# Finishing the results of a gated MLP by rows, and interleaving the first two units of each token block

## The chip, the cores and the metric

The kernel runs on one core of one Trainium2 chip. Its engines work side by side, each with its own queue: PE (TensorE) multiplies matrices into the accumulation memory (PSUM, eight banks), DVE (VectorE) and ACT (ScalarE) work element by element, POOL (GpSimd) and SP (SyncE) here only issue transfers between the chip's main memory and the on-chip memory. The metric is the time of one execution in device microseconds. Before the change it is 699.53 us, the median of three runs (698.68 to 700.48).

## The reference, cut to what matters

```python
x  = A_x                                   # 1 x 2048 x 512
xn = layernorm(x)
a, b = xn @ dft_hid_re.T, xn @ dft_hid_im.T
s  = dft_seq_re @ a - dft_seq_im @ b       # 2048 x 2048 matrices
h  = relu(xn @ w1 + b1) ** 2               # w1: 512 x 1792
g  = silu(h @ w2 + b2)                     # w2: 1792 x 512
return x + s * g
```

The change lies in the last two lines: `h @ w2`, the silu, the product with `s` and the sum with `x`.

## The kernel before, in words

Every matrix is float32. Each is split into a high and a low part (`split`, lines 68 to 76: ACT writes the high part, DVE the difference), and a product is three matmuls: high by high, high by low, low by high. On top of that the matrices are cut into two by two pieces and multiplied with seven products instead of eight (`PRODUCTS`, line 48). The four pieces of the result are put together from the seven products by `combine` (line 256): ACT copies product 1, then four DVE operations add and subtract the others, reading PSUM.

The stages are: layer norm and the sequence transform (up to about 408 us, with the hidden transform `stage2`, whose result `s` goes to main memory as `Y`), then MLP1 (`hidden`, 28 units, 420 to 549 us), which writes its squared results to main memory (`HD`), then MLP2 (the last loop, from line 815), in which the change lies.

MLP2 has 28 units. Unit n is token block c = n // 7 (512 tokens) and pair p = n % 7 (256 rows of w2). A unit does the seven products of its pair, 42 matmuls of 128 x 128 by 256 columns, through `add(k, p)` and `outer` (line 616), where k is the number of the product. All seven pairs of a block add up in the same seven accumulators, which take seven PSUM banks; so a new block can write a bank only when the last block's `combine` has read it. Products 2, 5 and 4 start from the bias, which ACT writes into the bank (`bias`, line 610). The order of products is `ORDER` (line 50), in the first unit of a block `FIRST`, and `FIRST_LAST` in the last block (lines 52, 53).

The left operand of unit n, `ready[c, p]`, lies in one of three places (`sixth(5 + n % 3, 2)`), so it can be made only when unit n - 3 no longer reads its own. It takes three steps (`operand`, line 589), which `go` calls by name: `h5` is the next step of unit 5's operand. They are a load from `HD` by SP, three DVE operations (`sums_a`, line 227), and the split into high and low. In unit n, behind its matmuls, `go` does the split of n + 2, the sums of n + 4 and the load of n + 6 (line 858). All engines work strictly in the order in which the program writes these calls (`manual_schedule`).

The right operands, the seven pairs of w2 in split form, lie in the places `W2_HOME` (line 511). Pairs 0, 1 and 6 are split in place; 2 to 5 are loaded in split form (`load_w2`, line 514, called as `l2` to `l5`). Pair `SHIFTED` is loaded in two pieces, and its seventh block (product 4's) lies `LINE` = 16 elements further on than it would otherwise.

After pair 6 of a block, `combine` writes the four result pieces to one buffer `e` (tag "e", one copy; the last block has its own, `g1a`). During the next block, `finish` (line 644) takes them one by one: silu on ACT (line 654), the product with `s` on DVE (line 658, `times`, with tiles loaded by `load_fin`), and a transfer on POOL (line 649) which adds the piece to the output. The output has held `x` since much earlier. A piece is one quarter of the block, 256 rows by 256 columns. The next `combine` may write `e` only when all four transfers have landed. The last block doesn't use `finish`: its matmuls of pairs 4 to 6 run product by product (`rest`, line 873), each piece is finished as soon as its products are done, and SP stores it.

Of the kernel before, what the change touches and what calls it, by code (L numbers as in the profile page):

```python
# [10 lines left out]
ALU = mybir.AluOpType  # L11

P = 128
S, D, F = 2048, 512, 1792
NS, ND, NF = S // P, D // P, F // P
NJ, NP = NS // 2, NF // 2
CW = 256
NC = S // CW
TC = 512
NTC = S // TC  # L20
# [4 lines left out]
REST = NP - 3  # L25
# [23 lines left out]

ORDER = (1, 2, 6, 7, 5, 3, 4)  # L50

FIRST = (1, 2, 6, 4, 7, 5, 3)
FIRST_LAST = (1, 2, 5, 4, 6, 7, 3)

B_SLOT = {B11: 0, B22: 1, B21: 2, T1: 3, T3: 4, T2: 5, T4: 6}
W1_SLOT = {A11: 0, A12: 1, A22: 2, S3: 3, S1: 4, S2: 5, S4: 6}
# [6 lines left out]
def fnet_gated_kernel(ctx, tc, x, xt, ct, wd, w1, w2, b1, b2, out):  # L63
    nc = tc.nc
# [22 lines left out]
    def bank(tag, name):  # L87

        n = {"b3": 3, "b2": 2}.get(tag, 1)
        return acc.tile([P, n, 512], F32, tag=tag, name=name)  # L90

    def buf(tag, shape, name, dtype=F32, bufs=1):
        return pool.tile(shape, dtype, tag=tag, bufs=bufs, name=name)
# [414 lines left out]
            nc.sync.dma_start(b.bitcast(F32), W1D[p][:, :, 3:7])  # L508
            W1[p] = [a[:, :, n] for n in range(3)] + [b[:, :, n] for n in range(4)]

    W2_HOME = "xc0", "xc1", 2, 3, 4, "wd0", "wd1"
    SHIFTED = 5

    def load_w2(p):
        to = W2_HOME[p]
# [94 lines left out]
    def bias(m, n, cols=slice(0, 2)):  # L610

        m = m.rearrange("p (k e) -> p k e", k=2)[:, cols]
        b = BIASED[n] * 256
        nc.scalar.activation(m, b2s[:, None, b:b + 256].to_broadcast([P, cols.stop - cols.start, 256]), AF.Copy)  # L614
# [13 lines left out]
    def at(src, k):  # L628

        h, b = WHERE[k]  # L630
        return src.rearrange("(h k p) (b e) -> h b p k e", h=2, k=2, b=2)[h, b]
# [9 lines left out]
                    nc.sync.dma_start(t[:, i].rearrange("p (k e) -> p k e", k=2), at(src, 2 * m + i))  # L641
                fin[c].append(t)

    def finish(c, e, k):

        silu(e, k)
        times(c, e, k)
        z = e[:, k].rearrange("p (k e) -> p k e", e=256)
        nc.gpsimd.dma_start(at(out[c * TC:(c + 1) * TC], k), z, accum_op=ALU.add)

    def silu(e, k, cols=slice(0, 2)):

        z = e[:, k, cols.start * 256:cols.stop * 256]
        nc.scalar.activation(z, z, AF.Silu)

    def times(c, e, k, cols=slice(0, 2)):
        w = slice(cols.start * 256, cols.stop * 256)
        nc.vector.tensor_tensor(e[:, k, w], e[:, k, w], fin[c][k // 2][:, k % 2, w], op=ALU.mult)
# [22 lines left out]
    for c, j in steps:  # L681
# [19 lines left out]
        if j == NJ - 1:  # L701
            e = buf("e", [P, 4, 512], f"c{c}")
# [4 lines left out]
        if c == NC - 1:  # L707

            if j == 2:
                e = buf("e", [P, 8, 256], "rows0")  # L710
# [24 lines left out]
    def go(*names):  # L735


        for v in names:
            k, n = v[0], int(v[1:])
            if k == "m":  # L740
                load_rows(n, buf("g1a" if n == 1 else "pq00", [P, 4, 256], f"rows{n}"))
            elif k == "l":
                load_w2(n)
            elif k != "h" or n < len(units):
                if v not in making:
                    making[v] = {"h": lambda: operand(n, *units[n]), "x": lambda: tokens(n // 2, n % 2),
                                 "w": lambda: late_w2(n)}[k]()
                next(making[v])
# [4 lines left out]
    def plan(c, p, ahead=(), behind=()):  # L753
        for n, names in enumerate((ahead, behind)):
            beside.setdefault((c, p), ([], []))[n].extend(names)
# [20 lines left out]
    plan(2, 6, ["h3"], ["h2"])  # L776
    plan(3, 0, [], ["w0"])
    plan(3, 1, ["w1", "l2"], ["h3"])
    plan(3, 2, ["l3"], ["w1"])
    plan(3, 3, [], ["w1"])  # L780
    plan(3, 4, ["l4", "w6"], ["h0"])
    plan(3, 5, ["h4"], ["h1"])
    plan(3, 6, ["h5"])

    with ordered:
        before = None
        for n, (c, p) in enumerate(units):
            ahead, behind = beside.get((c, p), ((), ()))
            go(*ahead)
            unit = hidden(n, c, p)  # L790
            next(unit)
            if n == 0:
                go("m1", "x2", "x3")
                for v in range(4, NP):
                    load_w1(v)
            if n == len(units) - 1:

                m26, m4 = bank("b2", "m_b2_o0"), bank("ba", "m_ba_o0")
                bias(m26[:, 0], 2)
                bias(m4[:, 0], 4)  # L800
            if before:
                next(before)
            next(unit)
            go(*behind)
            before = unit
            if n == 0:
                go(*["x2", "x3"] * 2)
                stage2(NC - 1, 0)
                stage2(NC - 1, 1, "ba")
                go("x2", "x3")  # L810
        m753, m1 = bank("b3", "m_b3_o0"), bank("bb", "m_bb_o0")
        bias(m753[:, 1], 5)
        next(before)

        for n, (c, p) in enumerate(units):
            last = c == NTC - 1
            if n == 0:
                ms = m26, m753, m4[:, 0], m1[:, 0]
                at_ = product
            elif not last and p == 0:  # L820

                m4, m26, m753, m1 = (bank(tag, f"m_{tag}_o{c}") for tag in (("bb", "ba")[c - 1], "b2", "b3", "bc"))
                ms = m26, m753, m4[:, 0], m1[:, 0]
                bias(ms[2], 4)
                bias(product(ms, 2), 2)
                bias(product(ms, 5), 5)
            elif p == 0:

                m5, m40 = (bank(tag, f"m_{tag}_last")[:, 0] for tag in ("bb", "bc"))
                m12, m67 = bank("b2", "m_12"), bank("b3", "m_67")  # L830
                m3 = bank("ba", "m_ba_last")[:, 0]
                m4 = m40, m67[:, 2]
                ms = {1: m12[:, 0], 2: m12[:, 1], 6: m67[:, 0], 7: m67[:, 1], 5: m5, 3: m3}
                at_ = dict.__getitem__
                bias(m5, 5)
                bias(m40, 4, slice(0, 1))
                bias(ms[2], 2)
                bias(m4[1], 4, slice(1, 2))

            def add(k, p):  # L840
                if last and k == 4:
                    for i in range(2):
                        outer(m4[i], k, ready[c, p], p, (i,))
                else:
                    outer(at_(ms, k), k, ready[c, p], p)

            go(*["l5"] * (n == 0))
            if not last or p < REST:
                for k in ORDER if p else FIRST_LAST if last else FIRST:
                    add(k, p)  # L850
            if n == 1:

                nc.scalar.activation(stats[:, 0, 0, 0:1], stats[:, 0, 0, 0:1], AF.Silu)
            if p == NP - 1 and not last:
                e = buf("e", [P, 4, 512], f"z{c}")
                combine(e, ms)
                done_next = c, e
            go(f"h{n + 2}", f"h{n + 4}", *["w6"] * (n in (0, 3)), f"h{n + 6}")
            if p == (3 if last else 5):
                load_fin(c)  # L860
            if p == NP - 1 and not last:
                done = done_next
            elif c:
                for k in ((2, 3), (0,), (1,), (), (), (), ())[p] if not last else ((), (0,), (1, 2), (3,), (), (), ())[p]:
                    finish(*done, k)


        e = buf("g1a", [P, 4, 512], f"z{c}")
        tail = NP - 1
        whole = slice(0, 512)  # L870
        w = [slice(i * 256, (i + 1) * 256) for i in range(2)]

        def rest(ks, ps=range(REST, NP)):
            for k in ks:
                for f in ps:
                    add(k, f)

        def step(to, a, b, op, w=whole):
            nc.vector.tensor_tensor(e[:, to, w], a[:, w], e[:, b, w], op=op)

        rest((1, 2, 6), range(REST, tail))
        rest((1, 2), (tail,))
        nc.scalar.activation(e[:, C21], ms[1], AF.Copy)
        step(C11, ms[2], C21, ALU.add)
        silu(e, C11)
        times(c, e, C11)
        plus(c, e, C11)
        rest((6,), (tail,))
        rest((7,))
        step(C22, ms[6], C21, ALU.add)  # L890
        step(C21, ms[7], C22, ALU.subtract)
        rest((5,))
        step(C12, m5, C22, ALU.subtract)
        step(C22, m5, C21, ALU.add)
        silu(e, C22)
        rest((3,))
        for f in range(REST, NP):
            outer(m4[0], 4, ready[c, f], f, (0,))
        times(c, e, C22)
        plus(c, e, C22)  # L900
        step(C12, m3, C12, ALU.add)
        silu(e, C12)
        step(C21, m4[0], C21, ALU.subtract, w[0])
        silu(e, C21, one)
        for f in range(REST, NP):
            outer(m4[1], 4, ready[c, f], f, (1,))
        times(c, e, C12)
        step(C21, m4[1], C21, ALU.subtract, w[1])
        silu(e, C21, two)
        times(c, e, C21, one)  # L910
        plus(c, e, C21, one)
        times(c, e, C21, two)
        plus(c, e, C21, two)
        plus(c, e, C12)
# [43 lines left out]
```

## Time and profile before

| | |
|---|---|
| median of three runs | 699.53 us (698.68 to 700.48) |
| the profiled execution | 698.08 us |
| its span, first to last instruction | 696.3 us |
| PE busy / DVE / ACT / POOL | 683.0 / 578.3 / 345.4 / 16.9 us |
| mean granted clock of TensorE | 0.997 |
| chain of waits, by engine | PE 89%, DVE 7%, issue 1%, DMA 1%, ACT 1% |
| MLP2, first matmul to last | 549.3 to 689.0 us |

The span is what lies between the first and the last instruction of one execution; the rest of the run's time lies outside. Engine times are busy times. In a row of a timeline come the start in us, the length in us, the engine, the line of the kernel, the operation, output <- input, the shape and how many instructions were merged into the row; in brackets how long the engine had been idle ahead of it, and what ended the wait. A row of transfers gives the count, the size of one, and the us from issue to landing.

### The profile page before, as it was taken

The numbers are of one execution on the slowest core, as the hardware profiler recorded it, in microseconds if no ns is written. First come the engines' busy times: TensorE is split into PE (matmuls) and PEld (weight loads), VectorE is DVE, ScalarE is ACT, GpSimd is POOL, SyncE is SP. The second block draws the span as 40 slices with busy tenths as digits, with TensorE's granted clock in tenths as the row PEclk, the third lists the DMA queues.
The fourth block names the chain that finished last, engine by engine and source line by source line (L and its number), as shares of the span: only waits on it lengthen the run. The fifth ranks groups of instructions, "written<-read, shape, count | busy, mean of one in ns | idle before, by whom it ended". The sixth has DMA issues, their size and how long they took to land.

```text
span 696.3 us, 12737 instructions
## 1 busy us (share of the span) xinstructions
PE 683.0 (98%) x5179; PEld 646.3 (93%) x5179; DVE 578.3 (83%) x866; ACT 345.4 (50%) x463; POOL 16.9 (2%) x20
## 2 busy tenths in 40 slices
PE   8999999999999999999999999999999999989995
PEld 5778889999999999999999989999999999989995
DVE  7998974579599598798797797989988699969885
ACT  3444634344353444444543326685867855344441
POOL 0000000000000000000000000000000100202011
PEclk9999999999999999999999999999999999999998
DMA  8622340734673763744835999374488954667674
GB/s 326 232 92 92 134 167 33 257 127 146 201 285 136 260 227 119 283 156 148 305 101 175 402 377 289 124 292 177 162 292 318 363 213 152 156 155 170 180 190 91
DMA packets 52250, 141.09 MB, mean 203 GB/s; under 512 B 4912, under 2 KB 18736, under 8 KB 50992
## 3 DMA queue, kind: packets, MB, share of 16 engines
q1 hardware_dynamic: 44896, 122.46, 50.5%
q10 hardware_dynamic: 3456, 12.58, 4.5%
q0 software_dynamic: 3840, 5.24, 4.3%
q8 instruction: 40, 0.66, 0.4%
q14 instruction: 18, 0.15, 0.1%
HBM read 97.00 MB, written 46.42 MB: 206 GB/s over the span
## 4 chain that ended last, share of the span: by engine, by line
PE 89%; DVE 7%; issue 1%; DMA 1%; ACT 1%; POOL 0%; DVEq 0%; ACTq 0%; POOLq 0%
PE m_b L322 23%; PE yps L309 13%; PE hps L573 10%; PE pq_b L375 7%; PE m_b_o L621 7%; PE hps_b L573 5%; PE m_bb L322 5%; PE m_ba L322 5%; PE m L621 3%; PE hps_ba L573 3%; PE pq_ba L375 2%; DVE block L72 1%; PE hps_bb L573 1%; PE pq_bb L375 1%; PE m_ba_o L621 1%
## 5 line engine op out<-in xcount | busy, mean ns | idle before, releaser
L322 PE MATMUL m_b<-g,block 128*128 128x256 f32 x1080 | 129.0, 276 | 0.0
L322 PEld LDWEIGHTS m_b<-g,block 128*128 128x128 f32 x1080 | 125.5, 188 | 0.1
L69 ACT ACTIVATE g<-raws 128x768 fp32r<-128x768 f32 (+2 forms) x65 | 57.4, 885 | 89.7 <-PE m_b L322 45.8
L72 DVE TENSOR_TENSOR g<-raws,g 128x768 fp32r<-128x768 f32 (+2 forms) x65 | 65.6, 1009 | 40.1 <-ACT g L69 40.0
L309 PE MATMUL yps<-wd,pq 128*128 128x512 f32 (+1 forms) x414 | 92.8, 374 | 0.0
L309 PEld LDWEIGHTS yps<-wd,pq 128*128 128x128 f32 x414 | 74.4, 188 | 13.7
L72 DVE TENSOR_TENSOR g<-sums,g 128x1024 fp32r<-128x1024 f32 x48 | 58.7, 1223 | 12.2 <-ACT g L69 12.2
L573 PE MATMUL hps<-xT,block 128*128 128x256 f32 x504 | 59.1, 276 | 0.0
L69 ACT ACTIVATE g<-sums 128x1024 fp32r<-128x1024 f32 x48 | 50.4, 1049 | 16.6 <-PE m_ba L322 7.8
L573 PEld LDWEIGHTS hps<-xT,block 128*128 128x128 f32 x504 | 58.0, 188 | 0.0
L375 PE MATMUL pq_b<-g,block 128*128 128x512 f32 x180 | 47.4, 395 | 0.5 <-DVE g L72 0.4
L621 PE MATMUL m_b_o<-w,block 128*128 128x256 f32 x360 | 43.9, 278 | 2.3 <-ACT m_b_o L614 2.3
L322 PE MATMUL m_b<-g,xc 128*128 128x256 f32 x360 | 45.0, 276 | 0.0
L621 PEld LDWEIGHTS m_b_o<-w,block 128*128 128x128 f32 x360 | 42.3, 188 | 2.8 <-ACT m_b_o L614 2.7
L322 PEld LDWEIGHTS m_b<-g,xc 128*128 128x128 f32 x360 | 42.8, 188 | 0.1
L375 PEld LDWEIGHTS pq_b<-g,block 128*128 128x128 f32 x180 | 33.3, 188 | 9.6 <-DVE block L72 2.1
L573 PE MATMUL hps_b<-xT,block 128*128 128x256 f32 x288 | 34.7, 276 | 0.0
L223 DVE TENSOR_TENSOR sums<-raws 128x512 f32<-128x512 f32 x49 | 33.7, 688 | 0.9 <-DMA raws<-in_ct 0.6
L69 ACT ACTIVATE block<-hr 128x1792 fp32r<-128x1792 f32 (+1 forms) x15 | 23.8, 1587 | 21.1 <-PE m_bb_o L621 6.5
L584 ACT ACTIVATE raws<-raws,b1s 128x512 f32<-128x512 f32 x42 | 28.1, 716 | 12.0 <-DVE raws L264 11.9
L573 PEld LDWEIGHTS hps_b<-xT,block 128*128 128x128 f32 x288 | 33.6, 188 | 0.0
L621 PE MATMUL m_b_o<-block 128*128 128x256 f32 x270 | 32.5, 278 | 0.0
(232 smaller groups left out, 1212.3 us busy)
## 6 DMA issues: line engine op xcount, KB each, us to landing
raws<-in_ct SPq DMA_DIRECT2D x63, 512.0 KB, 3.5
w1d<-w0g SPq DMA_DIRECT2D x21, 512.0 KB, 3.3
block<-w1d SPq DMA_DIRECT2D x6, 1792.0 KB, 9.1
hd<-raws ACTq DMA_DIRECT2D x18, 512.0 KB, 4.9
hr<-hd SPq DMA_DIRECT2D x15, 512.0 KB, 4.6
block<-w2d SPq DMA_DIRECT2D x3, 1792.0 KB, 15.5
y<-ysb SPq DMA_DIRECT2D x16, 256.0 KB, 3.2
fin<-y SPq DMA_DIRECT2D x16, 256.0 KB, 5.4
```

Source lines behind the costliest of these rows:

```text
L69: nc.scalar.activation(hi, src, AF.Copy)
L72: return nc.vector.tensor_tensor(lo, src, hi.bitcast(F32), op=ALU.subtract)
L223: nc.vector.tensor_tensor(t[:, 0:2], r[:, 0:1].to_broadcast([P, 2, 256]), r[:, 1:3], op=ALU.add)
L309: nc.tensor.matmul(ps[:, s], PQ[c, m, k // 2][:, a_, w:w + P], WD[m, k][:, b_, s], start=n == 0, stop=n > len(todo) - 3, skip_group_check= ...
L322: nc.tensor.matmul(ps[:, d * CW:(d + 1) * CW], w[:, a_, d * P:(d + 1) * P], mv(b_), start=first and d == 0 and (a_, b_) == (HI, HI), stop= ...
L375: nc.tensor.matmul(accs[c][k], w, g[:, b_, 2 * h:2 * h + 2], start=j == 0 and h == 0 and (a_, b_) == (HI, HI), stop=j == NJ - 1 and h == 1 ...
L573: nc.tensor.matmul(product(ms, k), W1[p][a][:, a_, q * P:(q + 1) * P], xT[c, q][:, b_, b], start=share not in first, stop=q == 1 and (a_, ...
L584: nc.scalar.activation(x_[:, s], x_[:, s], AF.Relu, bias=b1s[:, f:f + 1])
L621: nc.tensor.matmul(m[:, k * 256:(k + 1) * 256], g[:, a_, a, k * P:(k + 1) * P], W2[p][b][:, b_], start=p == 0 and k == 0 and (a_, b_) == ( ...
```

## The change

Three edits, all in MLP2.

*Order of products.* The first two units of a block are taken together, by `GROUPS`. A block's entry lists groups of products. In unit 0 only the first group is done, with pair 0; in unit 1 the first group with pair 1, and then each further group with pair 0 and with pair 1. Block 0 has the groups (1, 2, 6, 4), (7, 5, 3); blocks 1 and 2 have (1, 4), (2, 6), (7, 5, 3); block 3 has (5), (1, 2), (4, 6, 7, 3). At the end of a block the split of the operand after next (`h{n + 2}`) is called ahead of `combine`; for the last block the bank of product 5 gets its bias there too.

*Results by rows.* `finish` takes two pieces at a time, those of the same 256 rows, in units 1 and 2 of the next block. After their silus and products it issues two transfers, each of 128 whole rows (512 columns). So there still are four accumulating transfers of 256 KB for a block, on POOL. Before, pieces 2 and 3 were finished in unit 0, 0 in unit 1 and 1 in unit 2 (in the last block: 0 in unit 1, 1 and 2 in unit 2, 3 in unit 3).

*Shifted block.* The pair in two pieces with the shifted block is now pair 3, which takes the place `wd0`; pairs 4 and 5 move to the places 3 and 4. `wd0` becomes free only at the end of MLP1, so pair 3 is loaded at the start of MLP2 (`l3` where `l5` was), and pairs 4 and 5 during MLP1 where 3 and 4 were.

```diff
-FIRST = (1, 2, 6, 4, 7, 5, 3)
-FIRST_LAST = (1, 2, 5, 4, 6, 7, 3)
+GROUPS = ((1, 2, 6, 4), (7, 5, 3)), *[((1, 4), (2, 6), (7, 5, 3))] * 2, ((5,), (1, 2), (4, 6, 7, 3))
...
-    W2_HOME = "xc0", "xc1", 2, 3, 4, "wd0", "wd1"
-    SHIFTED = 5
+    W2_HOME = "xc0", "xc1", 2, "wd0", 3, 4, "wd1"
+    SHIFTED = 3
...
-    def finish(c, e, k):
-
-        silu(e, k)
-        times(c, e, k)
-        z = e[:, k].rearrange("p (k e) -> p k e", e=256)
-        nc.gpsimd.dma_start(at(out[c * TC:(c + 1) * TC], k), z, accum_op=ALU.add)
+    def finish(c, e, h):
+
+        for k in (2, 0) if h == 0 else (1, 3):
+            silu(e, k)
+            times(c, e, k)
+        for k in range(2):
+            n = c * TC + (1 - h) * 256 + k * P
+            nc.gpsimd.dma_start(out[n:n + P].rearrange("p (b e) -> p b e", b=2), e[:, h:4:2, k * 256:(k + 1) * 256],
+                                accum_op=ALU.add)
...
-    plan(3, 2, ["l3"], ["w1"])
+    plan(3, 2, ["l4"], ["w1"])
...
-    plan(3, 4, ["l4", "w6"], ["h0"])
+    plan(3, 4, ["l5", "w6"], ["h0"])
...
-                m5, m40 = (bank(tag, f"m_{tag}_last")[:, 0] for tag in ("bb", "bc"))
+                m40 = bank("bc", "m_bc_last")[:, 0]
...
-                bias(m5, 5)
...
-            go(*["l5"] * (n == 0))
-            if not last or p < REST:
-                for k in ORDER if p else FIRST_LAST if last else FIRST:
+            go(*["l3"] * (n == 0))
+            if p < 2:
+                groups = GROUPS[c]
+                for k in groups[0]:
+                    add(k, p)
+                for ks in groups[1:] if p else ():
+                    for f in (0, 1):
+                        for k in ks:
+                            add(k, f)
+            elif not last or p < REST:
+                for k in ORDER:
                     add(k, p)
...
             if p == NP - 1 and not last:
+                go(f"h{n + 2}")
+                if c == NTC - 2:
+                    m5 = bank("bb", "m_bb_last")[:, 0]
+                    bias(m5, 5)
                 e = buf("e", [P, 4, 512], f"z{c}")
                 combine(e, ms)
                 done_next = c, e
-            go(f"h{n + 2}", f"h{n + 4}", *["w6"] * (n in (0, 3)), f"h{n + 6}")
+            go(*[f"h{n + 2}"] * (p < NP - 1 or last), f"h{n + 4}", *["w6"] * (n in (0, 3)), f"h{n + 6}")
...
-                for k in ((2, 3), (0,), (1,), (), (), (), ())[p] if not last else ((), (0,), (1, 2), (3,), (), (), ())[p]:
-                    finish(*done, k)
+                if p in (1, 2):
+                    finish(*done, p - 1)
```

## The prediction

> **What bounds the kernel now.** I read the page first, then the chain of waits, then the timeline of each engine over MLP2 (549 us to the end), since every edit lies there.
>
> ```profile
> span 696.3 us, 12737 instructions
> ...
> 611.71 6.21 DMA out<-z
> 618.53 1.69 ACT block L69
> 621.28 1.64 PE m_b_o L621 x12
> ```
>
> In MLP2 the chain is mostly PE's matmuls, but at 611.71 it leaves PE for a result transfer of 6.21 us, and comes back only at 621.28. PE's timeline shows what that cost, and two more losses:
>
> ```profile
> 549.33 0.84 PE L621 MATMUL m_bb_o<-w,block 128*128 128x256 f32 x6
> ...
> 552.93 2.32 PE L621 MATMUL m_b_o<-w,block 128*128 128x256 f32 x18 [0.72 <-ACT m_b_o L614]
> ...
> 586.45 2.39 PE L621 MATMUL m_b_o<-w,block 128*128 128x256 f32 x18
> ...
> 599.27 3.70 PE L621 MATMUL m_b_o<-block 128*128 128x256 f32 x30
> ...
> 614.11 3.56 PE L621 MATMUL m_b_o<-w,block 128*128 128x256 f32 x30
> ...
> 618.68 0.97 PE L621 MATMUL m_bc_o<-w,block 128*128 128x256 f32 x6 [0.33 <-ACT z L261]
> 621.28 1.64 PE L621 MATMUL m_b_o<-w,block 128*128 128x256 f32 x12 [1.62 <-ACT m_b_o L614]
> ...
> 635.68 3.56 PE L621 MATMUL m_b_o<-block 128*128 128x256 f32 x30
> ...
> 656.62 2.03 PE L621 MATMUL m<-w,block 128*128 128x256 f32 x15
> ...
> 688.17 0.87 PE L621 MATMUL m<-w,block 128*128 128x256 f32 x6
> ```
>
> One matmul lasts 0.28 us and the next starts before its end, so 30 in 3.56 us are 29 steps of 0.1133; 30 in 3.70 are steps of 0.118. The slow step holds from 586.45 to about 614.1 and from 656.62 to the end, each time from a pause of under 0.3 us on; after the pauses at 552.93 and 621.28, over 0.6 us, the step is the quick one. In block 1 the slow step ends where the shifted weight block (pair 5, product 4) has been used. A unit of 42 matmuls is 4.76 us quick, 4.94 slow. PE ends at 688.17 + 0.87 = 689.04; 28 quick units without a pause from 549.33 would end at 682.6.
>
> Now the result transfers on POOL, with DVE's last products of the first pair ahead of them, the landing of the first, and two copies on the same queue (their line is 586):
>
> ```profile
> 540.24 0.71 POOL L586 DMA_DIRECT2D hd<-raws  x1 [539.79 <-ACT raws L585]
> 544.99 0.56 POOL L586 DMA_DIRECT2D hd<-raws  x1 [4.04 <-ACT raws L585]
> ...
> hd<-raws POOLq DMA_DIRECT2D x1, 512.0 KB, 9.1
> ...
> 593.32 1.29 DVE L658 TENSOR_TENSOR z<-z,fin 128x512 f32<-128x512 f32 x2
> ...
> 594.36 1.25 POOL L649 DMA_DIRECT2D out<-z  x1 [38.31 <-DVE z L658]
> 600.64 1.20 POOL L649 DMA_DIRECT2D out<-z  x1 [5.03 <-DVE block L72]
> ...
> out<-z POOLq DMA_DIRECT2D x1, 256.0 KB, 6.0
> ```
>
> Both products are done at 594.61, and yet the second transfer starts at 600.64, 0.28 us after the first has landed (594.36 + 6.0). The copies don't do this: the second is issued at 544.99, while the first lands at 549.3. I read it so that an accumulating transfer keeps POOL's queue until it has landed. Releasers given for these rows (a DVE split) are not it: what the transfer needs was there.
>
> ```profile
> 611.71 1.18 POOL L649 DMA_DIRECT2D out<-z  x1 [4.03 <-issue]
> 631.20 1.19 POOL L649 DMA_DIRECT2D out<-z  x1 [18.30 <-DVE z L658]
> ...
> 644.63 1.19 POOL L649 DMA_DIRECT2D out<-z  x1 [3.35 <-issue]
> 668.26 1.20 POOL L649 DMA_DIRECT2D out<-z  x1 [22.44 <-DVE z L658]
> ...
> 683.21 1.19 POOL L649 DMA_DIRECT2D out<-z  x1 [3.21 <-DVE z L658]
> ...
> out<-z POOLq DMA_DIRECT2D x1, 256.0 KB, 5.5
> ...
> out<-z POOLq DMA_DIRECT2D x1, 256.0 KB, 4.6
> ```
>
> A set of four so takes, first issue to last landing: 611.71 + 6.21 - 594.36 = **23.6** us; 644.63 + 5.5 - 631.20 = **18.9**; 683.21 + 4.6 - 668.26 = **19.6**. Mean 20.7. Until the set has landed its buffer z is taken, and the next block's combine cannot begin:
>
> ```profile
> 618.03 0.60 ACT L261 ACTIVATE z<-m_bc_o 128x512 f32<-128x512 f32 x1 [7.74 <-DMA out<-z]
> 650.25 0.60 ACT L261 ACTIVATE z<-m_bc_o 128x512 f32<-128x512 f32 x1 [3.89 <-PE m_bc_o L621]
> ...
> 618.66 1.23 DVE L262 TENSOR_TENSOR z<-m_b_o,z 128x1024 f32<-128x1024 f32 x1 [4.79 <-ACT z L261]
> ...
> 623.19 2.02 DVE L72 TENSOR_TENSOR block<-raws,block 128x1792 fp32r<-128x1792 f32 x1
> 625.12 0.69 DVE L229 TENSOR_TENSOR hr<-hr 128x512 f32<-128x512 f32 x1
> ...
> 626.64 2.02 DVE L72 TENSOR_TENSOR block<-sums,block 128x1792 fp32r<-128x1792 f32 x1
> ...
> 672.42 2.02 DVE L72 TENSOR_TENSOR block<-hr,block 128x1792 fp32r<-128x1792 f32 x1
> ```
>
> From these, start to start: copy to combine 0.63, combine 4.53, a split 1.93, the sums of one operand 1.52. Two result products take 1.2 by the row at 593.32. DVE works a whole unit's 3.45 us out of 4.76, and around a combine it is late.
>
> **The change part by part.** *Interleaving.* No matmul is added or taken away. In block 0 products 7, 5 and 3 come 24 matmuls later, so the pause of 0.72 goes: with its restart 1.0 us. Blocks 1 to 3 start with products whose banks are free first, and the short pauses at 586 and 656 go, and with them the slow step: 27.5 x 0.0047 / 0.118 = 1.1 us, and 32.4 us by the same share, 1.3 us. The 1.62 at 621.28 is covered by 12 more matmuls (1.36) ahead of it. With the 0.33 and the restarts, all that interleaving can give is 689.04 - 682.9 (28 units and the last matmul's length) = 6.1 us. It asks the second operand of a block earlier; moving that split ahead of the combine (on DVE 1.93, on ACT 1.7) supplies it, and makes the combine begin later.
>
> *Shifted block.* One pair 3 load now is due at unit 3 and not unit 5:
>
> ```profile
> 549.56 1.30 SPq L524 DMA_DIRECT2D w<-w2d  x2
> ...
> w<-w2d SPq DMA_DIRECT2D x1, 1536.0 KB, 10.6
> ```
>
> It lands at about 560.2; unit 3 starts at 549.33 + 3 x 4.76 = 563.6, so it is hidden by 3.4 us (the smaller second piece feeds only product 4, 4.1 us later). Without that cover it costs what it is late. The loads of pairs 4 and 5 start on SP's queue where those of 3 and 4 did, and are due later: nothing. Where a slow step does set in, it now ends two units sooner (0.4 us), and in block 3 at all.
>
> *Finishing by rows.* Activations, products and bytes stay. The first transfer of a set now waits for two products, in unit 1 of the block and not unit 0: that is later. The transfer's shape, 128 rows of two 1 KB pieces, has no row here; I bound it by 18.9 and 23.6 a set and take the mean, since number, bytes and queue are the same and I see no reason that the queue is released earlier. The Trainium skill speaks against that reading: "DMA: Bandwidth & Descriptors", section "Two DMAs through the same engine are not ordered", has descriptors of one queue start in order but pipelined. By that rule a second transfer would follow at once, and the sum would be that of the first rival; the two rows at 594.36 and 600.64 disagree.
>
> **The sum.** DVE before the first combine ends a sum at 580.6 (old combine 581.24 after 0.61 idle). Split 582.5, combine 587.1, then sum, split, sum, split, sum, two products: 3 x 1.52 + 2 x 1.93 + 1.2 = 9.6, so 596.7. Transfer 0.4 later: **597.1**, against 594.36. Set: 617.8. Copy 617.9, where it was 618.03. Combine 618.5 to 623.1; 9.6 and 0.4: second set from 633.1 (was 631.20) to **653.8**. Old: 650.1, and the copy at 650.25 waited for PE, not for the set; now it waits for the set. PE starts block 2 at 618.6 and without the 1.62 pause finishes at 651.9; product 5 of two units (12 matmuls) covers to 653.3, then it waits for the combine's first step, 653.9 + 0.63 + 1.23 = 655.8: 2.5 us. That is where the stall goes. Combine ends at 659.1. From there DVE has four sums, four splits and four products up to the operand of pair 5: 6.1 + 7.7 + 2.4 = 16.2, so 675.3 (old: 672.42 + 2.02 = 674.4). PE arrives after 8 of the last 126 matmuls, at about 674.4, and waits 0.9. Then 118 x 0.1133 + 0.28 = 13.7: **689.0**, as before. After PE nothing changes (its last products go through DVE in the same order). The profiled execution is 698.08, 1.45 under the median of 699.53; a change of 0.0 puts the median at **699.5**.
>
> What interleaving wins on PE is so held back by two sets of four transfers in a row. The end moves by the sum of both sets: 1 us a set is 2 us. So the landing time of a transfer decides, and with it what else is loading:
>
> ```profile
> 600.63 0.32 SPq L598 DMA_DIRECT2D raws<-hd  x1
> ...
> 644.92 0.32 SPq L598 DMA_DIRECT2D sums<-hd  x1
> ```
>
> Loads issued next to the transfers at 600.64 and 644.63, which both needed 5.5 us; the median of all is 4.7.
>
> **The rivals.** *1, the queue isn't held* (other pieces, or the hold was something else). Both sets land long before they matter, PE runs through: 682.9, gain 6.1, **693.4**. For it: the copies. Against: every transfer of the three sets starts as the one before lands. *2, quick sets.* With 18.9 both, 3.6 us come off: **696.0**. For: whole rows of 2 KB lie together; two of three sets are under 20. Against: the later start puts the third transfer of each set beside a load (splits end, and loads start, at 603.7 and 607.2 by my sum, the third transfer at about 607). *3, slower: each transfer of both sets meets loads*, as in the first set. With 23.6 both, 5.8 come on top: **705.3**. It decides from 21.7 a set (2.1 us in all). For: the fourth of each set falls beside the loads of the next results. Against: only one set of three was so long. The idle time at block 2 would be 5.4 us. The Trainium skill, "TensorE: Matmul & The Clock Gate", section "What's actually happening", halves the clock after an idle window of about 3.4 us; no pause in MLP2 here is so long, and it would add to this rival alone. *4, the slow step stays.* If the new order leaves short pauses, four units a block at 0.18 us more: up to 2.2 us, **701.7**, if they lie where PE is the bound.
>
> **How the numbers follow.** About 0.3% (2.1 us) is what a measurement of this kernel can tell from no change. Forecast 0.42; rival 1 0.13; 2 0.22; 3 0.18; 4 0.05. Faster: rivals 1 and 2, 0.35. Slower: 3 and half of 4, 0.21. The forecast's own range is 697.4 to 701.6; with rivals 1 and 2 whole and the milder part of 3, 693.0 to 704.0.
>
> **What will show it.** Rows of POOL: if two accumulating transfers of a set overlap, rival 1; the set's length from first issue to last landing, against 20.7, says 2 or 3. ACT's copy rows of blocks 1 and 2: both should end on the transfer, at 618 and 654. PE's row of block 3 should show a pause of 2 to 3 us after product 5, and one near 1 us at the operand of pair 5. Groups of 30 should read 3.56 throughout. A first transfer before 595, or a combine that doesn't wait, would make the prediction wrong.

## The result, and the profile after

The changed kernel takes **705.51 us** (median of six runs, 704.22 to 708.54); the kernel before, run beside it, 700.00 (six runs, 698.62 to 701.62). The ratio is 1.0085, with a 95% interval of 1.0062 to 1.0109: slower, by about 6 us. The forecast was 699.5 and no change; the result lies above its upper bound of 704.0 and at the number of rival 3 (705.3). In the profiled executions the time went from 698.08 to 705.54 us. In the changed kernel the product loop is line 620, the transfer line 650, ACT's copy line 260.

The page of the changed kernel, its span and its chain of waits:

```profile
span 703.8 us, 12738 instructions
...
PE 76%; DVE 14%; DMA 4%; issue 4%; ACT 2%; POOL 0%; DVEq 0%; ACTq 0%; POOLq 0%
```

PE had 89% of the chain before. Now DVE, transfers and "issue" have 22% together: the end is set in part by something else than matmuls. PE's timeline of MLP2 shows where:

```profile
549.73 0.84 PE L620 MATMUL m_bb_o<-w,block 128*128 128x256 f32 x6
...
585.81 6.96 PE L620 MATMUL m_b_o<-w,block 128*128 128x256 f32 x60
607.61 3.56 PE L620 MATMUL m_b_o<-block 128*128 128x256 f32 x30
620.64 1.58 PE L620 MATMUL m_bc_o<-w,block 128*128 128x256 f32 x6 [4.03 <-ACT z L260]
...
632.88 3.70 PE L620 MATMUL m_b_o<-block 128*128 128x256 f32 x30
...
662.23 4.34 PE L620 MATMUL m<-w,block 128*128 128x256 f32 x24 [4.33 <-ACT m L613]
...
696.01 0.52 PE L620 MATMUL m<-w,block 128*128 128x256 f32 x3
```

Blocks 0 and 1 run without a pause. The starts of blocks 2 and 3 wait for over 4 us each, and both rows behind a wait are far too long: six matmuls took 1.58 us where six otherwise take 0.84. The table by stretches gives the granted clock. A row has the stretch, its length, the busy time and count of PE, its weight loads, DVE, ACT and POOL, and then three numbers: granted clock, DMA share, GB/s.

```profile
620.60:624.20 3.60, 3.56 (x17) 3.56 (x18) 3.44 (x3) 1.09 (x2) 0.00 (x0) 0.53 0.00 0
624.20:632.00 7.80, 7.80 (x68) 7.80 (x68) 5.94 (x10) 4.04 (x4) 0.00 (x0) 1.00 0.25 68
...
662.20:664.90 2.70, 2.67 (x12) 2.67 (x13) 2.56 (x4) 0.68 (x2) 0.00 (x0) 0.50 0.00 0
```

After each pause the clock is at half (0.53, 0.50) for some 3 us, then full again. That is the rule which the prediction set beside rival 3 (the Trainium skill, "TensorE: Matmul & The Clock Gate", section "What's actually happening": half the clock after an idle window of about 3.4 us); the trace agrees, with waits of 4.03 and 4.33 us (rows above).

What the pauses wait for is in ACT's timeline, the copy at each block's start:

```profile
620.00 0.60 ACT L260 ACTIVATE z<-m_bc_o 128x512 f32<-128x512 f32 x1 [6.45 <-DMA out<-z]
...
659.69 0.60 ACT L260 ACTIVATE z<-m_bc_o 128x512 f32<-128x512 f32 x1 [5.74 <-DMA out<-z]
```

It is the last transfer of a set. POOL's timeline, then the us from issue to landing of the transfers at 607.02, 613.55 and 652.67, then SP's loads beside them:

```profile
597.73 1.14 POOL L650 DMA_DIRECT2D out<-z  x1 [41.27 <-DVE z L660]
602.37 1.09 POOL L650 DMA_DIRECT2D out<-z  x1 [3.50 <-issue]
607.02 1.09 POOL L650 DMA_DIRECT2D out<-z  x1 [3.56 <-issue]
613.55 1.07 POOL L650 DMA_DIRECT2D out<-z  x1 [5.44 <-issue]
637.09 1.09 POOL L650 DMA_DIRECT2D out<-z  x1 [22.47 <-DVE z L660]
...
652.67 1.08 POOL L650 DMA_DIRECT2D out<-z  x1 [5.26 <-issue]
```

```profile
out<-z POOLq DMA_DIRECT2D x1, 256.0 KB, 6.2
out<-z POOLq DMA_DIRECT2D x1, 256.0 KB, 6.3
...
out<-z POOLq DMA_DIRECT2D x1, 256.0 KB, 6.9
```

```profile
607.45 3.78 SPq L597 DMA_DIRECT2D hr<-hd  x2
611.28 2.64 SPq L640 DMA_DIRECT2D fin<-y  x4
...
651.16 1.97 SPq L640 DMA_DIRECT2D fin<-y  x4
```

The first two transfers of both sets needed 4.2 to 4.4 us. The first set lasts 613.55 + 6.3 - 597.73 = 22.1 us, the second 652.67 + 6.9 - 637.09 = **22.5** (forecast 20.7 each). The long ones stand beside loads: the fourth of each set starts within 2.3 us after four loads of `s` (`fin`, 1 MB), which `load_fin` issues in unit 5. The third of each (6.2 and 6.0 us) stands beside an operand's loads (`hr`).

**Where PE's time went.** From the start of each matmul to the next, all that lies above the quick step of 0.1133 us, summed over MLP2 and sorted by the length of the step; an experiment's row is explained below:

| kernel | last matmul starts | pauses (over 0.25 us) | steps of 0.19 to 0.25 us: half clock, and one restart behind each pause | slow steps (0.118) |
|---|---|---|---|---|
| before | 688.8 | 3.3 us | 0.6 us | 2.4 us |
| changed | 696.2 | 9.2 | 2.8 | 1.3 |
| rows alone | 698.6 | 9.7 | 4.1 | 2.2 |
| changed, loads of `s` later | 688.2 | 4.6 | 0.3 | 0.2 |
| order alone | 683.2 | 0 | 0 | 0.2 |
| changed, eight half transfers | 682.7 | 0 | 0.1 | 0.2 |

Changed against before: 0.4 later start + 5.8 of pauses + 2.2 in the half clock's column - 1.0 of slow steps = 7.4 us, which is the difference of the first column. The columns are not independent causes: time that PE loses in block 2 can shorten the wait at block 3.

### The profile page after: what moved, and what is told of

Read it like the earlier page. It is cut to its first block, busy times and chain, and to the rows that moved or that the text cites. A ratio compares the mean times of both kernels' runs of the same rounds, so it can differ in the third digit from the quotient of the medians.

```text
span 703.8 us, 12738 instructions
## 1 busy us (share of the span) xinstructions
PE 684.7 (97%) x5179; PEld 648.1 (92%) x5179; DVE 578.7 (82%) x866; ACT 346.1 (49%) x463; POOL 15.6 (2%) x20
## 4 chain that ended last, share of the span: by engine, by line
PE 76%; DVE 14%; DMA 4%; issue 4%; ACT 2%; POOL 0%; DVEq 0%; ACTq 0%; POOLq 0%
PE m_b L321 21%; PE yps L308 12%; PE hps L572 9%; PE pq_b L374 7%; PE hps_b L572 5%; PE m_bb L321 4%; PE m_ba L321 4%; DVE block L71 4%; PE m L620 3%; PE hps_ba L572 3%; DMA out<-z 2%; PE pq_ba L374 2%; DMA raws<-in_xt 1%; PE pq_bb L374 1%; PE hps_bb L572 1%
```

## The experiments

Beside these runs the kernel before took 698.1, 698.7 and 697.2 us on the three occasions (13, 27 and 24 runs); ratios are to it. **Theory A**: the four accumulating transfers follow one another, late and beside loads, and their length sets the end. **Rivals**: the new order, the shifted block, or the slow matmuls have a cause of their own.

### One part at a time

*Order and shift, finishing as before* (`finish` itself as it was, too).

```diff
-                if p in (1, 2):
-                    finish(*done, p - 1)
+                for k in ((2, 3), (0,), (1,), (), (), (), ())[p] if not last else ((), (0,), (1, 2), (3,), (), (), ())[p]:
+                    finish(*done, k)
```

> The changed kernel with finishing as before the change (a piece at a time, in units 0, 1 and 2), so only the interleaving and the shifted block are new. Theory (an accumulating transfer holds POOL's queue, and the set of four that starts later keeps z too long): the first transfer of block 0's set starts near 593.5 instead of 597.7, the set lands by 612 to 617, PE's pause ahead of block 2 is under 1.5 us instead of 4.3, none reaches 3.4 us, and the run takes 694 to 698 us, faster than before. Rival (the interleaving itself costs the time): it stays near 705.

Measured: 693.93 us (692.89 to 697.55), ratio 0.9952 (0.9929 to 0.9976). One pause is left:

```profile
616.60 0.97 PE L620 MATMUL m_bc_o<-w,block 128*128 128x256 f32 x6 [0.60 <-ACT z L260]
```

The first set still takes 22.8 us here (593.03 to 615.8), no less than the 22.1 of the changed kernel, but it begins 4.7 us sooner, and the second (19.3 us) begins 9.8 us sooner. So the length of the sets hurts because finishing by rows starts them later.

*Rows alone, in the kernel before* (the same lines the other way round, and the two transfers of 128 rows).

> The kernel before with only finishing by rows in units 1 and 2. Theory: the first set starts near 598.5 instead of 594.4 and lands near 621, the second near 660; both combines wait for it, so the run takes 706 to 712 us, slower than the changed kernel too, since nothing covers the bias any more. Rival (interleaving at fault, rows harmless): 699 to 701.

Measured: 706.55 us (702.73 to 708.06), ratio 1.0108 (1.0067 to 1.0149). PE's waits at blocks 2 and 3 grow from 0.33, 1.62 and under 0.3 to:

```profile
622.77 1.04 PE L621 MATMUL m_bc_o<-w,block 128*128 128x256 f32 x6 [3.47 <-ACT z L261]
625.37 2.93 PE L621 MATMUL m_b_o<-w,block 128*128 128x256 f32 x12 [1.56 <-ACT m_b_o L614]
...
663.64 2.24 PE L621 MATMUL m<-w,block 128*128 128x256 f32 x12 [2.97 <-ACT m L614]
```

Behind the wait of 2.97 us come six quick matmuls and then 15 at 0.214 us each. So the clock was halved after less idle time than the window of about 3.4 us of the Trainium skill ("TensorE: Matmul & The Clock Gate", section "What's actually happening"); the measurement decides.

*Order alone* (the first experiment with the shifted block back in pair 5).

> The kernel before with the new order of products (and the split ahead of the combine) and nothing else: finishing a piece at a time, shifted block in pair 5. Theory (the order is what gains, the shift adds little): the pauses of 0.72 us in block 0 and of under 0.3 at block 1 are gone, the one of 1.6 at block 2 is gone or under 1; where a slow step sets in it ends at pair 5 and not at pair 3. Run 694 to 695, up to 1 us over the order with the shift (693.93). Rival (the two only gain together): 697 to 699.

Measured: 693.36 us (692.31 to 698.43), ratio 0.9947 (0.9917 to 0.9976). No pause is left in MLP2, and nearly all its steps are quick (row in the table; 29 slow ones).

*Shift alone* (with the loads of pairs 3, 4 and 5 at the places that go with it).

```diff
-    W2_HOME = "xc0", "xc1", 2, 3, 4, "wd0", "wd1"
-    SHIFTED = 5
+    W2_HOME = "xc0", "xc1", 2, "wd0", 3, 4, "wd1"
+    SHIFTED = 3
```

> The kernel before with the shifted weight block moved to the fourth weight pair, and nothing else. Theory (the shift is worth little by itself; the loss is in the transfers): the slow step of block 1 ends at unit 3 and not unit 5, two units of 0.18 us, about 0.4 us; in block 3 it ends at unit 3, four units sooner than the end, 0.6 to 0.7 us. Transfers start as before (594 to 595, 631), the copy at 618 still ends on a transfer. Run 697 to 698, 0.5 to 1 us under before, too little to tell from no change. Rival (the early load of pair 3 is late and is what the change loses on): a wait of PE for a weight block in unit 3 of block 0, run over 700.

Measured: 698.32 us (697.11 to 702.23), ratio 0.9993 (0.9969 to 1.0016): no difference that can be told. The rival (a late weight load) has nothing for it: no wait at pair 3.

What follows: the order gains some 4 us, the shift nothing that can be told, and the finishing by rows loses 7.5 us in the kernel before and some 9 on top of order and shift, more than the gain.

### What makes the transfers follow one another

*Copies.* The transfers of blocks 0 to 2 write the product without adding `x`.

```diff
-            nc.gpsimd.dma_start(out[n:n + P].rearrange("p (b e) -> p b e", b=2), e[:, h:4:2, k * 256:(k + 1) * 256],
-                                accum_op=ALU.add)
+            nc.gpsimd.dma_start(out[n:n + P].rearrange("p (b e) -> p b e", b=2), e[:, h:4:2, k * 256:(k + 1) * 256])
```

> The changed kernel, its result transfers of blocks 0 to 2 plain copies on the same queue, shape and order: the sum with x is left out for these three blocks. Theory (accumulating is what holds the queue): the two transfers of a unit start 1.1 to 1.3 us apart, a set takes under 11 us, no PE pause at blocks 2 and 3, run 692 to 695 us. Rival (the queue is held by 256 pieces, however they are written): turns of 4.4 to 6.5 us and about 705 as now.

Measured: 692.29 us (691.84 to 692.67), ratio 0.9922 (0.9899 to 0.9944). No pause is left at blocks 2 and 3, and two transfers start together, by POOL's timeline:

```profile
597.54 1.41 POOL L650 DMA_DIRECT2D out<-z  x2 [41.20 <-DVE z L659]
```

The software queue's row (packets, MB, share) in the ten us from 597 on, first with the copies, then in the changed kernel:

```profile
q0 software_dynamic: 320, 1.05, 35.5%
```

```profile
q0 software_dynamic: 544, 0.52, 45.4%
```

The copies carry four transfers in 320 packets, 80 each; accumulating, two transfers took 544, 272 each. So this experiment changes two things at once, the adding and the number of packets.

*Eight transfers of half the size*, all accumulating:

```diff
-            nc.gpsimd.dma_start(out[n:n + P].rearrange("p (b e) -> p b e", b=2), e[:, h:4:2, k * 256:(k + 1) * 256],
-                                accum_op=ALU.add)
+            for b in range(2):
+                nc.gpsimd.dma_start(out[n:n + P, b * 256:(b + 1) * 256], e[:, h + 2 * b, k * 256:(k + 1) * 256],
+                                    accum_op=ALU.add)
```

> The changed kernel, each transfer cut in two (128 rows by 256 columns, 128 pieces of 1 KB, eight to a block). If any accumulating transfer holds the queue until it has landed: eight turns of 3.3 us or more, a set of 27 to 35 us, and a run well above 710. If it is the number of pieces (256) that fills the queue: several are in flight at once, starts 1 us apart, and the run takes 693 to 698.

Measured: 692.18 us in one run, and repeated:

> The changed kernel with eight transfers of half the size a block (128 rows by 256 columns each), once more for an interval, since it was the quickest kernel so far: 691.9 to 692.6, ratio to the kernel before 0.990 to 0.993. PE runs through blocks 1 to 3 but for 0.16 us at the operand of pair 5 in the last block.

Measured: 693.55 us (691.89 to 695.82, seven runs), ratio 0.9928 (0.9900 to 0.9955): the ratio as expected, the time a little above. POOL's rows of the first set, from the first of the two:

```profile
597.17 2.68 POOL L651 DMA_DIRECT2D out<-z  x3 [41.21 <-DVE z L661]
600.44 0.84 POOL L651 DMA_DIRECT2D out<-z  x1 [0.59 <-issue]
```

Three are issued one behind the other, though they need 4.9 us to land (median of four). The fourth starts 0.3 us after the first has landed (597.17 + 3.0 us). So "an accumulating transfer keeps the queue until it has landed" fell. The packets of the eight transfers of the second set, with the row of these transfers:

```profile
q0 software_dynamic: 1152, 1.05, 43.0%
...
out<-z POOLq DMA_DIRECT2D x8, 128.0 KB, 4.7
```

That is 144 packets each. Three are 432 packets in flight, and a fourth would make 576; two whole ones would make 544. A limit between 432 and 544 packets explains both. A limit in bytes doesn't: two copies in flight are 512 KB, as two whole accumulating transfers would be. That points to room in the queue rather than to the adding.

*More room.* The scratch of the software queue is doubled; the space comes from keeping only the first half of `b2` and using it for both halves of the result.

```diff
-    nc = bacc.Bacc("TRN2", target_bir_lowering=False, num_devices=1, dynamic_dma_scratch_size=1024)
+    nc = bacc.Bacc("TRN2", target_bir_lowering=False, num_devices=1, dynamic_dma_scratch_size=2048)
```

> The changed kernel with twice the room for the software queue's descriptors (the program's scratch for dynamic transfers, 1024 to 2048); the room is found by keeping only the first half of the MLP2 bias and using it for both halves, so the second 256 columns of the result get a wrong bias. No instruction is added or taken away but one half of a bias load. Theory (a transfer of 256 pieces with accumulation fills the queue's room, and so the next must wait until it has landed): with twice the room two or more of a set are in flight together, as in the run with eight half transfers; POOL rows of one set start within 10 us, sets are done before 612 and 650, no pause of PE at blocks 2 and 3, run 692 to 694. Rival (accumulation of a 256-piece transfer holds the queue however much room there is): POOL starts follow each landing by 0.3 us, pauses of 3 to 5 us at blocks 2 and 3, run 704 to 707.

Measured: 692.82 us (692.36 to 694.61), ratio 0.9913 (0.9877 to 0.9950). The changed kernel's own transfers now go in pairs:

```profile
597.50 2.22 POOL L650 DMA_DIRECT2D out<-z  x2 [41.20 <-DVE z L660]
602.22 2.19 POOL L650 DMA_DIRECT2D out<-z  x2 [2.49 <-DVE z L660]
```

No pause of PE is left at blocks 2 and 3. With nothing else changed but half a bias (the second 256 columns of the result get the wrong one), this shows the cause: the room for descriptors, which one accumulating transfer of 256 pieces fills to more than a half. In the third set the third transfer goes out at 668.1 us, while two are under way (they land at 668.7 and 670.0), and the fourth 0.3 us after the first of them has landed. So three (816 packets) fit and four (1088) don't: with twice the scratch, about twice the limit. The Trainium skill ("DMA: Bandwidth & Descriptors", section "Terms") has the software queue write its descriptors to rings on the chip, which fits; how many fit, the runs alone show.

### What makes a transfer long, and what the clock adds

*The loads of `s` later*, at the start of the next block:

```diff
+            if p == 0 and c:
+                load_fin(c - 1)
...
-            if p == (3 if last else 5):
+            if p == 3 and last:
                 load_fin(c)
```

> The changed kernel with the loads of s for blocks 0 to 2 (four of 256 KB each) issued at the start of the next block instead of in unit 5; nothing else. In the changed kernel they are issued at 611.3 and 651.2, just ahead of the fourth transfer of each set, which needs 6.3 and 6.9 us and not 4.2. Theory (loads beside a transfer make it longer, and the sets' length decides the end): the fourth transfer meets less, 5 us or under, each set 1 to 1.5 us shorter (21 instead of 22.1 and 22.5), the end 2 to 3 us sooner: run 702.5 to 704. The third transfers (6.2 and 6.0, beside an operand's load) stay as they are. Rival (the fourth transfer is long for a reason of its own, such as the operand's load ahead): sets of 22 and more, run 705 to 706.

Measured: **697.01** us (696.39 to 699.62), ratio 0.9983 (0.9959 to 1.0007). That is 8 us between the profiled executions (705.54 and 697.61) for moved loads, far more than expected, and no longer slower than the kernel before. POOL's timeline, the us to landing of the fourth transfer (the same in both sets), and PE's waits:

```profile
597.91 1.14 POOL L650 DMA_DIRECT2D out<-z  x1 [41.27 <-DVE z L660]
...
613.32 1.07 POOL L650 DMA_DIRECT2D out<-z  x1 [5.21 <-issue]
633.14 1.09 POOL L650 DMA_DIRECT2D out<-z  x1 [18.75 <-DVE z L660]
...
648.87 1.08 POOL L650 DMA_DIRECT2D out<-z  x1 [5.84 <-issue]
```

```profile
out<-z POOLq DMA_DIRECT2D x1, 256.0 KB, 4.3
```

```profile
618.36 0.97 PE L620 MATMUL m_bc_o<-w,block 128*128 128x256 f32 x6 [1.56 <-ACT z L260]
...
655.81 2.99 PE L620 MATMUL m<-w,block 128*128 128x256 f32 x24 [2.44 <-ACT m L613]
```

The fourth transfer of both sets now lands in 4.3 us, the sets last 19.7 and 20.0. The third transfers, beside an operand's loads that were not moved, still need 6.0 and 6.6 us; that these loads make them long is not tested. The rest of the 8 us is what hung on the long sets: with pauses of 1.6 and 2.4 us the clock stays full and the slow step doesn't set in (table: 2.5 and 1.1 us less), and the second set starts at 633.14, 4 us sooner, of which the first set's length gives only 2.4.

*The pause filled with matmuls.* 34 matmuls into the free bank of product 4 ahead of its bias, at the start of block 2 alone; block 3 is the control.

```diff
+                for _ in range(34 if c == 2 else 0):
+                    nc.tensor.matmul(ms[2][:, 0:256], ready[c - 1, 6][:, HI, 0, 0:P], W2[6][0][:, HI],
+                                     start=True, stop=True, skip_group_check=True)
```

> The changed kernel with 34 extra matmuls into the free bank of product 4 at the start of block 2 (the bias then overwrites them, so the result stays what it was): PE is busy for some 3.9 us of the 4.3 us in which it otherwise stands. Block 3 is left as it is, as the control. Theory (a pause of over 4 us halves the clock, and the first 15 matmuls then take 213 ns each and not 113 to 118): the matmuls of block 2 start at full speed, 15 x 0.1 = 1.5 us less there, while block 3 still shows some 11 at 213 ns after its pause; how much reaches the end depends on the second set, which begins after block 2's combine and not by PE: run 704 to 705.5, at most 1.5 us under the changed kernel. Rival (the slow matmuls after the pause wait for something else, a split or a bank): they stay slow in block 2 too.

Measured: 703.94 us (703.00 to 705.38), ratio 1.0066 (1.0044 to 1.0089). The stretches behind the two points:

```profile
620.50:624.00 3.50, 3.47 (x31) 3.28 (x30) 3.00 (x3) 1.53 (x3) 0.00 (x0) 1.00 0.02 8
...
660.40:663.60 3.20, 3.20 (x16) 3.20 (x16) 3.03 (x5) 1.43 (x2) 0.00 (x0) 0.50 0.00 0
```

Clock 1.00 and 31 matmuls in 3.5 us where PE had been kept busy, 0.50 and 16 in 3.2 where it hadn't: the slow matmuls come from the pause. The half clock also costs work that isn't on PE. In the changed kernel DVE waits for an ACT split that waits for PE:

```profile
620.62 1.23 DVE L261 TENSOR_TENSOR z<-m_b_o,z 128x1024 f32<-128x1024 f32 x1 [5.03 <-ACT z L260]
...
631.92 2.02 DVE L71 TENSOR_TENSOR block<-hr,block 128x1792 fp32r<-128x1792 f32 x1 [1.58 <-ACT block L68]
```

```profile
630.19 1.70 ACT L68 ACTIVATE block<-hr 128x1792 fp32r<-128x1792 f32 x1 [3.43 <-PE m_b_o L620]
```

From this combine's first step to the next set it is 637.09 - 620.62 = 16.5 us; with the pause filled the same steps take 14.7:

```profile
620.86 1.23 DVE L261 TENSOR_TENSOR z<-m_b_o,z 128x1024 f32<-128x1024 f32 x1 [4.87 <-PE m_ba_o L827]
...
635.60 1.09 POOL L650 DMA_DIRECT2D out<-z  x1 [21.01 <-DVE z L660]
```

So the theory's doubt whether the gain would reach the second set is answered: the set starts 1.5 us sooner. The two medians were taken beside different runs of the kernel before, and their intervals overlap; the mechanism rests on the traces.

### One that told nothing

*Eight half transfers, and the last block's finishing one unit later.*

```diff
-                if p in (1, 2):
-                    finish(*done, p - 1)
+                if p - last in (1, 2):
+                    finish(*done, p - last - 1)
```

> The run with eight half transfers a block, with one edit more: the last block finishes its predecessor's result in units 2 and 3 and not 1 and 2, so that the products of the result stand behind more of the splits on DVE. Theory (in block 3 the DVE chain of combine, sums, splits and products up to the operand of pair 5 is the bound for 0.16 us, and that pause brings on the slow step of 118 ns for the last 115 matmuls): the pause goes, the step stays at 113 ns to the end, run 691 to 692, 0.5 us less than with eight half transfers alone (692.18 in one run). Rival (the same products are only paid later, at the end): 692 to 693, with the idle time at a later operand.

Measured: 692.50 us (691.89 to 697.12), ratio 0.9912 (0.9883 to 0.9940), which can't be told from the eight transfers alone. The pause at the operand of pair 5 is gone, but another of 0.40 us stands at the start of block 3, with slow steps behind it. The best kernels with the full result are those at 692 to 694 us: order alone, order with shift, and the eight transfers, all under the kernel before and the changed one. Which of them is best, these runs don't tell.

## Why the prediction was wrong

**Right: the place and the form of the stall.** The first transfer was put at 597.1 and started at 597.73, with MLP2 itself 0.4 later. Both copies end on the transfer, as forecast; the waits of blocks 0 and 1 are gone; block 3 stops after product 5. The W2 load stays hidden, as the run with the shift alone shows too. All that the order can give was put at 6.1 us, with a last matmul ending at 682.9; with the order alone MLP2 begins 0.5 later, and the last matmul starts at 683.2 and ends 0.3 after that. That a transfer of whole rows lasts as long as one of the old pieces held too: the quickest of either kind need 4.1 us.

**Wrong: "I bound it by 18.9 and 23.6 a set and take the mean".** This is the term that failed first. The sets took 22.1 and 22.5, above the 21.7 from which rival 3 was to decide. The prediction had the reasons in hand (third transfer at about 607 beside a load; "the fourth of each set falls beside the loads of the next results") and put 0.18 on them. The mean mixed unlike sets: in the kernel before, the loads of `s` run from 612.75 beside the fourth transfer of the first set (23.6 us), and only from 648.82, 1.3 us ahead of the landing, in the second (18.9). Moving this group of loads in the changed kernel gave 19.7 and 20.0, and the forecast's own sum with these (1.7 less, and a first transfer 0.8 later) is 688.1; the last matmul ended at 688.4, with a pause of 2.4 at block 3 (2.5 forecast). The steps behind the set were sound as long as the clock was whole; the set itself was mis-sized by 1.4 and 1.8 us.

**Wrong: one for one, with the clock at nothing.** "The end moves by the sum of both sets" makes 3.2 us; the last matmul ended at 696.5, 7.5 after the forecast. Along the chain these are the first transfer (0.6 later), the first set (1.4 longer), the way from its landing to the next set (17.2 us for 15.3), the second set (1.8 longer), and the way from its landing to the last matmul's end (36.9 us for 35.2). The two ways, 1.9 and 1.7, are what the sum lacked. Both begin with PE at half clock. Where the clock stayed whole they are as forecast: the first took 15.5 us both with the pause filled and with the loads later, the second 35.3 with the loads later. On the first way DVE's splits wait for ACT's, and these for PE; on the second, how much is the half clock and how much the slow step wasn't separated. The prediction set the clock beside rival 3, as an addition to it, and gave it no price.

**Wrong: when the slow step sets in.** I had it that pauses over 0.6 us are followed by the quick step. The run with rows alone has the very pause of 0.72 us of the kernel before, at the same place, and now the slow step behind it, 2.39 us for the 18 matmuls that took 2.32:

```profile
552.91 2.39 PE L621 MATMUL m_b_o<-w,block 128*128 128x256 f32 x18 [0.72 <-ACT m_b_o L614]
```

"Groups of 30 should read 3.56 throughout" failed as well (3.70 at 632.88): in the changed kernel some 150 slow steps follow the pause at block 2, once the clock is full again; with the loads later, quick steps follow waits of 1.6 and 2.4 us. What decides it stays open. That it ends at the shifted block held (642 in the changed kernel). The wait of near 1 us at the operand of pair 5 didn't come: in the changed kernel no step of PE from 663 on is over 0.25 us.

**Wrong in its reason: "an accumulating transfer keeps POOL's queue until it has landed".** For this shape it held at all nine turns, so the sum wasn't harmed. But it is the number of packets against the room in the queue. Had I seen that, halving the transfers would have been an edit to propose; and rival 1 ("other pieces") was weighed by the wrong question.

**Rival 3 came true by number** (705.3 against 705.5), partly by accident: its price was 23.6 a set without the clock; the sets were shorter and the half clock made up for it.

## What to carry to other kernels

Price a chain of transfers at the place where the change puts it, with the loads that will be issued beside it, and not by the mean of where it stood before. When a buffer is released by such a chain, ask whether the wait can reach some 3 us on TensorE: here 2.44 us left the clock whole and 2.97 us halved it, and behind the pauses of over 4 us the rest of the chain took 1.7 to 1.9 us more than forecast, partly since the engines that wait for PE are late as well. Where transfers of a software queue follow one another without a reason in the data, count packets in flight against the queue's room: smaller transfers, or more room, took the whole stall away here.

## What the runs showed of the chip that I had not expected

- The room in the software queue: 432 packets in flight went, 544 did not, with the scratch at 1024; at 2048, three accumulating transfers of 272 packets went together (816) and a fourth did not.
- A plain copy of the same 256 KB is 80 packets, an accumulating transfer 272; one of half the size is 144.
- Four loads of 256 KB issued just ahead lengthen an accumulating transfer from 4.3 to 6.3 and 6.9 us.
- Moving those loads to the start of the next block changed the profiled execution by 8 us, of which the two sets themselves are 2.4 and 2.5.
